# Six PSUM banks as six tiles, and the gate copy ahead of the last exponentials

## The chip, the core and the metric

One core of one Trainium2 chip runs the whole program in one launch. The metric is the device time of one execution in microseconds. PE is TensorE, DVE is VectorE, ACT is ScalarE, POOL is GpSimd, SP is the engine that issues most DMAs.

## What is computed

Block-causal attention over 8 batches of 8 heads (576 positions, head size 64, blocks of 64), then a layer of 8 experts of which each row takes the one with the highest logit:

```
scores = (q @ k.T) / 8                       # per batch and head, 576 x 576
scores = where(i // 64 >= j // 64, scores, -1e9)
attn = exp(scores - max(scores)); attn /= sum(attn) + 1e-9
x = (attn @ v), heads side by side           # 4608 rows of 512
logits = x @ w_gate + modality_bias[modality_id]
e = argmax(logits);  gate = softmax(logits)[e]
out[row] = gate * (relu(x[row] @ w1[e]) @ w2[e])
```

## The kernel before, in words

**Attention.** Two heads of a batch form a pair; there are 32 pairs, and one slot of the program's order handles one. Queries are cut into nine subtiles of 64 rows (subtile s sees 64 (s + 1) keys), and both heads of the pair lie side by side on the 128 partitions. The scores of all nine subtiles fill six PSUM banks, which are one tile, `wide`, of 6 x 512 columns; `COL` (line 48) gives each subtile's first column. Subtile 8 lies across two banks.

The order of the instructions on every engine is written by hand: `ORDER` (line 62) lists the steps of a slot, each with the stage it belongs to (0: this slot's pair, 1: the pair before, -2: a load two pairs ahead). The steps are

- S0 to S3, the scores of a piece (line 188, PE); M0 to M4, the negated maxima of a unit of subtiles (line 193, DVE); E0 to E4, the exponentials (line 199, ACT). E4 handles subtiles 3, 8 and 1.
- G, nine small matmuls of the values with the gate's weights (line 221, PE), and g, the copy of their result out of PSUM next to the values (line 224, ACT). L loads queries and keys two pairs ahead (line 169, SP); values and their transposes come by lines 173 and 174.
- Va and Vb, the attention weights of the pair before times its values (line 233, PE): Va subtiles 0 to 6, Vb 7 and 8. Vb writes the bank that G wrote, and waits for g. Za and Zb normalize their results (lines 245 to 248, DVE).
- T0 to T6, transposes of the exponentials in groups of up to four (line 209, PE), each group into one of the six banks, and C0 to C6, the copies out (line 214; 1, 3 and 5 on DVE, the others on ACT).
- the q steps place the routing of a finished batch between them, a step or two at a time.

The scheduling layer that turns this into a program puts in the waits. It does so by tiles and what is known of each access to them.

**Experts.** `Experts` takes rows in groups of 256: `fetch` gathers them (line 620, POOL), `turn_rows` transposes them (line 633) and splits them in a high and a low part (636 ACT, 637 DVE), `up_products` makes four groups of 24 products (line 651), each evicted by `up_relu` (657 ACT, 658 DVE), `down` makes two groups of 24 (line 697), which line 699 (ACT) scales and line 700 (POOL) scatters. A step is one such group of rows. There are nine steps of the first expert, eight and a short one of the second, one of the third. The products rotate over banks 0 to 2, the turns over banks 3 and 4, and the second `down` group uses bank 5.

Of the kernel before, what the change touches and what calls it, by code (L numbers as in the profile page):

```python
# [11 lines left out]
F32 = mybir.dt.float32  # L12
F32R = mybir.dt.float32r
BF16 = mybir.dt.bfloat16
I32 = mybir.dt.int32
AF = mybir.ActivationFunctionType
ALU = mybir.AluOpType
AX = mybir.AxisListType
# [4 lines left out]
B, H, S, D = 8, 8, 576, 64  # L23
# [3 lines left out]
NSUB = S // D  # L27
# [17 lines left out]
GATE = (NSUB - SEVEN) * VW  # L45
TABLE = GATE + 5 * 2 * NE
UNITS = ((7,), (6, 0), (5,), (4, 2), (3, 8, 1))
COL = {7: 0, 6: 512, 0: 960, 5: 1024, 4: 1536, 2: 1856, 3: 2048, 8: 2304, 1: 2880}
FLIP = (6, 0, 5, 4, 2)
PIECES = (((7, 0, 512),), ((6, 0, 448), (0, 0, 64)), ((5, 0, 384), (3, 0, 256)), ((8, 0, 256), (4, 0, 320), (8, 256, 576), (2, 0, 192), (1, 0, 128)))  # L50
OFF = [32 * s * (s + 1) for s in range(NSUB)]
# [8 lines left out]
PARTS = (("idf", (128,)), ("ii", (128,)), ("iom8", (NE,)), ("iom40", (5, NE)), ("iov40", (5, NE)), ("inv5", (5,)), ("first5", (NE, 5)), ("base8", (NE,)), ("edges", (N // SLOT,)))  # L60

ORDER = (
# [3 lines left out]
)  # L66

# [35 lines left out]
def attention_moe(ctx, tc, qk, vr, vt, gmw, mid, mb, w1, w2, cf, ci, ld, out):  # L103
    nc = tc.nc
    pe, act, dve, pool = nc.tensor, nc.scalar, nc.vector, nc.gpsimd
# [14 lines left out]
    gm = cst.tile([128, PPB, 2 * NE], F32, name="gm")  # L120
    scratch = cst.tile([128, 1024], F32, name="scratch")
    zeros = scratch[:, 0:256].bitcast(BF16)
    lead = cst.tile([128, 128], BF16, name="lead")
    ones = cst.tile([128, 128], BF16, name="ones")
    run = cst.tile([128, NE], F32, name="run")
# [3 lines left out]
    bias = cst.tile([128, B * 5, NE], F32, name="bias")  # L129
# [8 lines left out]
    sml = ctx.enter_context(tc.tile_pool(name="sml", bufs=4, side="right"))  # L138
    att = att_stack.enter_context(tc.tile_pool(name="att", bufs=1, side="right"))
    ps = ctx.enter_context(tc.tile_pool(name="ps", bufs=1, space=PSUM))  # L140

    wide = ps.tile([128, 6 * 512], F32, name="wide")
    banks = [wide[:, 512 * i : 512 * i + 512] for i in range(6)]
    o0, b0 = (ps.tile([128, 512], F32, name=n) for n in ("o0", "b0"))
    raws = [att.tile([128, 2 * S], F32, name=f"raw{i}") for i in range(2)]
    q8s = [att.tile([128, S], F32, name=f"q8{i}") for i in range(2)]
# [29 lines left out]
    def scale(p):  # L176
        d = pairs[p]
        (pool if p else dve).tensor_scalar(d.q, d.raw[:, 0:S], SCALE, None, ALU.mult)  # L178

    def scores(p, u):  # L180
        d = pairs[p]
        if u == 0:
            d.nm = sml.tile([128, NSUB], F32, name="nm")
        for s, a, b in PIECES[u]:
            for h in range(2):
                t = h ^ (s in FLIP)
                hs = slice(64 * h, 64 * h + 64)
                pe.matmul(wide[64 * t : 64 * t + 64, COL[s] + a : COL[s] + b], d.q[hs, D * s : D * s + D], d.k[hs, a:b], start=True, stop=True)  # L188

    def maxima(p, u):  # L190
        d = pairs[p]
        for s in UNITS[u]:
            dve.tensor_reduce(d.nm[:, s : s + 1], wide[:, COL[s] : COL[s] + D * (s + 1)], AX.X, ALU.max, negate=True)  # L193

    def exps(p, u):
        d = pairs[p]
        for s in UNITS[u]:
            n = D * (s + 1)
            act.activation(d.pm[:, OFF[s] : OFF[s] + n], wide[:, COL[s] : COL[s] + n], AF.Exp, bias=d.nm[:, s : s + 1], scale=1.0)  # L199

    def height(g):
        return 64 if g >= HALF else 128
# [199 lines left out]
    def emit(name, p):  # L402
        one = {
            "L": lambda: load(p), "G": lambda: gates(p), "g": lambda: keep_gates(p), "Va": lambda: values(p, 0, SEVEN), "Vb": lambda: values(p, SEVEN, NSUB),
            "Za": lambda: rows(p, o0, 0, SEVEN), "Zb": lambda: rows(p, b0, SEVEN, NSUB),
        }
        if name in one:
            one[name]()
        else:
            dict(S=scores, M=maxima, E=exps, T=transposes, C=copies)[name[0]](p, int(name[1:]))  # L410
# [441 lines left out]
```

## Time and profile before

| what | value |
|---|---|
| median of 3 runs (lowest, highest) | 1529.61 us (1524.93, 1530.62) |
| the profiled run's own time | 1524.37 us |
| its span | 1522.6 us |
| PE busy with matmuls | 1033.8 us, 68% of the span |
| DVE, ACT, POOL busy | 380.8, 315.8, 216.5 us |
| mean granted TensorE clock | 0.784 |

Times inside the profile are microseconds from the start of the span. The granted clock is a share of 2.4 GHz: 1.00 is 2.4 GHz, 0.50 is 1.2 GHz. "Idle before" a group is the time in which its engine did nothing just before its instructions, and behind the arrow stands what ended that time.

### The profile page before, as it was taken

How to read it: one execution, taken by the hardware profiler on the slowest of the kernel's cores; microseconds unless marked ns; L12 is line 12 of the kernel's file. 1: busy time of each engine (PE TensorE's matmuls, PEld its weight loads, DVE VectorE, ACT ScalarE, POOL GpSimd, SP SyncE). 2: the span in 40 equal slices, each digit the busy share in tenths (PEclk: the TensorE clock that was granted, in tenths of full speed). 3: DMA queues.
4: the chain of work that ended last, by engine and by line, in shares of the span. 5: the costliest groups of instructions: out<-in, count | busy, mean ns of one | idle time of the engine just before them, and what ended most of it. 6: DMA issues, size and time to landing. Idle time of an engine off the chain costs nothing. (4 is left out here: it accounts for less than half of the span.)

```text
span 1522.6 us, 20688 instructions
## 1 busy us (share of the span) xinstructions
PE 1033.8 (68%) x8696; PEld 775.3 (51%) x8696; DVE 380.8 (25%) x995; ACT 315.8 (21%) x622; POOL 216.5 (14%) x177
## 2 busy tenths in 40 slices
PE   5656666556666665666656677777777777777776
PEld 2434434334344343343433466666666666666665
DVE  2322322323323233243322322111111111111110
ACT  2222222222222222222222211111111111111111
POOL 1000000101001010012242004111211111110100
PEclk6765666766657676666766779999999999999989
DMA  3123213113113113124333012111121011111000
GB/s 105 56 66 105 63 37 81 51 33 88 44 35 94 35 49 80 36 60 110 99 94 96 4 46 53 42 49 42 44 68 42 29 56 49 49 56 35 23 14 17
DMA packets 82623, 85.11 MB, mean 56 GB/s; under 512 B 53002, under 2 KB 64970, under 8 KB 82528
## 3 DMA queue, kind: packets, MB, share of 16 engines
q1 hardware_dynamic: 75040, 64.24, 15.5%
q0 software_dynamic: 7488, 19.52, 4.0%
q8 instruction: 69, 1.13, 0.3%
q14 instruction: 26, 0.21, 0.0%
HBM read 62.09 MB, written 22.25 MB: 55 GB/s over the span
## 5 line engine op out<-in xcount | busy, mean ns | idle before, releaser
L209 PE MATMUL wide<-cf,pm 128*128 128x128 f32 (+1 forms) x800 | 176.9, 353 | 152.7 <-DVE pt L214 81.6
L188 PE MATMUL wide<-raw,q 64*64 64x256 f32 (+7 forms) x1280 | 193.7, 689 | 122.4 <-ACT pm L199 113.2
L209 PEld LDWEIGHTS wide<-cf,pm 128*128 128x128 f32 (+1 forms) x800 | 103.7, 163 | 219.4 <-DVE pt L214 114.9
L193 DVE TENSOR_REDUCE nm<-wide 128x1 f32<-128x512 f32 (+8 forms) x288 | 129.6, 487 | 338.6 <-PE wide L188 286.8
L199 ACT ACTIVATE pm<-wide,nm 128x512 f32<-128x512 f32 (+8 forms) x288 | 138.0, 525 | 360.9 <-DVE nm L193 352.4
L188 PEld LDWEIGHTS wide<-raw,q 64*64 64x64 f32 x1280 | 84.9, 208 | 226.1 <-ACT pm L199 158.2
L651 PE MATMUL wide<-extra 128*128 128x256 f32 x960 | 127.4, 290 | 47.6 <-DVE extra L658 40.0
L658 DVE SCALAR_TENSOR_TENSOR extra<-wide,extra 128x512 fp32r<-128x512 f32 x72 | 49.8, 692 | 437.6 <-ACT extra L657 437.6
L178 POOL TENSOR_SCALAR q<-raw 128x576 f32<-128x576 f32 x31 | 51.2, 1650 | 689.3 <-DMA raw<-qk 666.1
L651 PEld LDWEIGHTS wide<-extra 128*128 128x128 f32 x960 | 119.5, 194 | 56.9 <-DVE extra L658 45.7
L214 ACT COPY pt<-wide 128x512 f32<-128x512 f32 (+1 forms) x128 | 64.5, 504 | 312.0 <-PE wide L209 312.0
L651 PE MATMUL wide<-extra,w0hb 128*128 128x256 f32 x512 | 95.7, 287 | 40.6 <-DVE extra L658 34.4
L214 DVE COPY pt<-wide 128x512 f32<-128x512 f32 (+1 forms) x96 | 66.1, 689 | 209.3 <-PE wide L209 209.3
L651 PEld LDWEIGHTS wide<-extra,w0hb 128*128 128x128 f32 x512 | 78.2, 188 | 48.9 <-DVE extra L658 39.2
L233 PE MATMUL o<-v,pt 128*64 128x73 f32 x2048 | 99.7, 267 | 0.0
L657 ACT ACTIVATE extra<-wide 128x512 fp32r<-128x512 f32 x72 | 43.0, 597 | 267.4 <-PE wide L651 266.6
L233 PEld LDWEIGHTS o<-v,pt 128*64 128x64 f32 x2048 | 94.9, 168 | 0.1
L233 PE MATMUL b<-v,pt 128*64 128x73 f32 x1152 | 44.8, 232 | 62.7 <-ACT v L224 62.7
L233 PEld LDWEIGHTS b<-v,pt 128*64 128x64 f32 x1152 | 40.0, 139 | 67.3 <-ACT v L224 67.3
L651 PE MATMUL wide<-extra,w0lb 128*128 128x256 f32 x256 | 71.7, 280 | 0.0
L697 PE MATMUL o<-extra 128*128 128x512 f32 x240 | 66.2, 436 | 0.0
L633 PE MATMUL wide<-cf,xr 128*128 128x128 f32 x148 | 33.0, 362 | 48.2 <-DVE extra L637 23.8
(142 smaller groups left out, 923.2 us busy)
## 6 DMA issues: line engine op xcount, KB each, us to landing
raw<-qk SPq DMA_DIRECT2D x31, 576.0 KB, 3.8
v<-vr SPq DMA_DIRECT2D x32, 320.0 KB, 3.8
vt<-vt SPq DMA_DIRECT2D x32, 288.0 KB, 4.0
xrows<-xr SPq DMA_DIRECT2D x16, 576.0 KB, 5.6
staging<-w SPq DMA_DIRECT2D x24, 256.0 KB, 4.5
staging<-w SPq DMA_DIRECT2D x12, 512.0 KB, 3.7
idlist<-btmp SPq DMA_DIRECT2D x8, 304.0 KB, 5.3
idlist<-idt,pi POOLq DMA_INDIRECT x40, 2.2
```

The costliest lines, as they stand in the source:

```text
L178: (pool if p else dve).tensor_scalar(d.q, d.raw[:, 0:S], SCALE, None, ALU.mult)
L188: pe.matmul(wide[64 * t : 64 * t + 64, COL[s] + a : COL[s] + b], d.q[hs, D * s : D * s + D], d.k[hs, a:b], start=True, stop=True)
L193: dve.tensor_reduce(d.nm[:, s : s + 1], wide[:, COL[s] : COL[s] + D * (s + 1)], AX.X, ALU.max, negate=True)
L199: act.activation(d.pm[:, OFF[s] : OFF[s] + n], wide[:, COL[s] : COL[s] + n], AF.Exp, bias=d.nm[:, s : s + 1], scale=1.0)
L209: pe.transpose(banks[GBANK[g]][0:m, 128 * i : 128 * i + 128], d.pm[:, o : o + m], idf)
L214: dve.tensor_copy(dst, src) if g in ON_DVE else act.copy(dst, src)
L233: pe.matmul(o[64 * h : 64 * h + 64], d.pt[:, a : a + 64], d.v[:, 5 * h + j, :], start=j == 0, stop=j == s // 2)
L633: nc.tensor.transpose(x[:, n * a + 128 * i : n * a + 128 * i + 128], s.xg[:, i, 128 * kc : 128 * kc + 128], self.idf)
L651: nc.tensor.matmul(hp[:, a, :], w[:, kc, ms], x[:, kc, :], start=i == 0, stop=i == len(mm) - 1)
L657: self.nc.scalar.activation(hh, hp, AF.Relu)
L658: self.nc.vector.scalar_tensor_tensor(hl, hp, 0.0, hh, ALU.max, ALU.subtract)
L697: nc.tensor.matmul(y, s.hs[m][x][:, ts], self.part(w, 1, m // 2)[:, m % 2, :], start=n == 0, stop=n == len(mm) - 1)
```

## The change

The six banks become six tiles, `bank0` to `bank5`, in the same places; `COL` names a bank and an offset in it. An instruction can then no longer reach over two banks, so subtile 8 is cut at key 256: its maximum is a reduction over the first 256 columns into a spare column of `nm`, and then one `tensor_scalar` over the other 320 that takes the smaller of the two negated maxima; its exponential is two instructions. The matmuls stay what they were: subtile 8 was already written in two pieces. In `ORDER`, E4 moves from ahead of G to behind g, so that ACT copies the gate's terms before the last exponentials.

```diff
-COL = {7: 0, 6: 512, 0: 960, 5: 1024, 4: 1536, 2: 1856, 3: 2048, 8: 2304, 1: 2880}
+COL = {7: (0, 0), 6: (1, 0), 0: (1, 448), 5: (2, 0), 4: (3, 0), 2: (3, 320), 3: (4, 0), 8: (4, 256), 1: (5, 320)}
+CUT = 256
 ...
-    ("S0", 0), ("S1", 0), ("M0", 0), ("qv", 1), ("E0", 0), ("S2", 0), ("M1", 0), ("E1", 0), ("S3", 0), ("M2", 0), ("E2", 0), ("M3", 0), ("E3", 0), ("M4", 0), ("E4", 0),
-    ("G", 0), ("L", -2), ("q1", 1), ("Va", 1), ("g", 0), ("q2", 1), ("q3", 1), ("Vb", 1), ("Za", 1), ("q4", 1), ("Zb", 1),
+    ("S0", 0), ("S1", 0), ("M0", 0), ("qv", 1), ("E0", 0), ("S2", 0), ("M1", 0), ("E1", 0), ("S3", 0), ("M2", 0), ("E2", 0), ("M3", 0), ("E3", 0), ("M4", 0),
+    ("G", 0), ("L", -2), ("q1", 1), ("Va", 1), ("g", 0), ("E4", 0), ("q2", 1), ("q3", 1), ("Vb", 1), ("Za", 1), ("q4", 1), ("Zb", 1),
 ...
+    dump = scratch[:, 256:512].bitcast(BF16)
 ...
-    wide = ps.tile([128, 6 * 512], F32, name="wide")
-    banks = [wide[:, 512 * i : 512 * i + 512] for i in range(6)]
+    banks = [ps.tile([128, 512], F32, name=f"bank{i}") for i in range(6)]
 ...
+    def place(s, a, b):
+        i, o = COL[s] if a == 0 else (COL[s][0] + 1, -CUT)
+        return banks[i][:, o + a : o + b]
+
+    def spans(s):
+        n = D * (s + 1)
+        return [(0, n)] if n <= 512 else [(0, CUT), (CUT, n)]
 ...
-                pe.matmul(wide[64 * t : 64 * t + 64, COL[s] + a : COL[s] + b], d.q[hs, D * s : D * s + D], d.k[hs, a:b], start=True, stop=True)
+                pe.matmul(place(s, a, b)[64 * t : 64 * t + 64], d.q[hs, D * s : D * s + D], d.k[hs, a:b], start=True, stop=True)
 ...
-            dve.tensor_reduce(d.nm[:, s : s + 1], wide[:, COL[s] : COL[s] + D * (s + 1)], AX.X, ALU.max, negate=True)
+            for a, b in spans(s):
+                low = d.nm[:, s : s + 1] if b == D * (s + 1) else d.nm[:, NSUB : NSUB + 1]
+                if a == 0:
+                    dve.tensor_reduce(low, place(s, a, b), AX.X, ALU.max, negate=True)
+                else:
+                    dve.tensor_scalar(dump[:, 0 : b - a], place(s, a, b), -1.0, d.nm[:, NSUB : NSUB + 1], ALU.mult, ALU.min, accum_out=low)
 ...
-            n = D * (s + 1)
-            act.activation(d.pm[:, OFF[s] : OFF[s] + n], wide[:, COL[s] : COL[s] + n], AF.Exp, bias=d.nm[:, s : s + 1], scale=1.0)
+            for a, b in spans(s):
+                act.activation(d.pm[:, OFF[s] + a : OFF[s] + b], place(s, a, b), AF.Exp, bias=d.nm[:, s : s + 1], scale=1.0)
```

What the built programs say of it is shown at three places on PE, with the waits that each instruction carries (the name in brackets is the engine or queue whose earlier work it waits for; line numbers of the changed kernel are 9 to 14 higher). The first is T0 to T6 of one slot, before:

```order
L209 MATMUL wide<-cf,pm_102 128x128 x4
L209 MATMUL wide<-cf,pm_102 128x128 [waits Activation_49]
L209 MATMUL wide<-cf,pm_102 128x128 x3
L209 MATMUL wide<-cf,pm_102 128x128 [waits DVE_49]
L209 MATMUL wide<-cf,pm_102 128x128 x3
L209 MATMUL wide<-cf,pm_102 128x128 [waits Activation_49]
L209 MATMUL wide<-cf,pm_102 128x128 x3
L209 MATMUL wide<-cf,pm_102 128x128 [waits DVE_49]
L209 MATMUL wide<-cf,pm_102 128x128 x3
L209 MATMUL wide<-cf,pm_102 64x128 [waits Activation_49]
L209 MATMUL wide<-cf,pm_102 64x128 x3
L209 MATMUL wide<-cf,pm_102 64x128 [waits DVE_49]
```

and of the changed kernel:

```order
L223 MATMUL bank_90<-cf,pm_108 128x128 x4
L223 MATMUL bank_91<-cf,pm_108 128x128 x4
L223 MATMUL bank_92<-cf,pm_108 128x128 x4
L223 MATMUL bank_93<-cf,pm_108 128x128 [waits Activation_49]
L223 MATMUL bank_93<-cf,pm_108 128x128
L223 MATMUL bank_93<-cf,pm_108 128x128 [waits Activation_49]
L223 MATMUL bank_93<-cf,pm_108 128x128
L223 MATMUL bank_94<-cf,pm_108 128x128 x3
L223 MATMUL bank_94<-cf,pm_108 128x128 [waits Activation_49]
L223 MATMUL bank_95<-cf,pm_108 64x128 x4
L223 MATMUL bank_90<-cf,pm_108 64x128 [waits Activation_49]
```

Before, each group carried a wait for the copy of the group ahead of it (ACT and DVE in turn). Now T0 to T2 carry none; the three waits in T3 and T4 are for exponentials of E4, and T6 waits for C0, which empties the bank it writes. The second place is S0 to S3, before:

```order
L188 MATMUL wide<-raw_93,q_95 64x512 [waits DMAHW1_49,Activation_49,Pool_49]
L188 MATMUL wide<-raw_93,q_95 64x512
L188 MATMUL wide<-raw_93,q_95 64x448 x2
L188 MATMUL wide<-raw_93,q_95 64x64 x2
L188 MATMUL wide<-raw_93,q_95 64x384 [waits Activation_49]
L188 MATMUL wide<-raw_93,q_95 64x384
L188 MATMUL wide<-raw_93,q_95 64x256 x2
L188 MATMUL wide<-raw_93,q_95 64x256 [waits Activation_49]
L188 MATMUL wide<-raw_93,q_95 64x256
L188 MATMUL wide<-raw_93,q_95 64x320 x4
L188 MATMUL wide<-raw_93,q_95 64x192 x2
L188 MATMUL wide<-raw_93,q_95 64x128 x2
```

and of the changed kernel:

```order
L197 MATMUL bank_90<-raw_98,q_100 64x512 [waits DMAHW1_49,Activation_49,Pool_49]
L197 MATMUL bank_90<-raw_98,q_100 64x512
L197 MATMUL bank_91<-raw_98,q_100 64x448 [waits DVE_49]
L197 MATMUL bank_91<-raw_98,q_100 64x448
L197 MATMUL bank_91<-raw_98,q_100 64x64 x2
L197 MATMUL bank_92<-raw_98,q_100 64x384 x2
L197 MATMUL bank_94<-raw_98,q_100 64x256 x4
L197 MATMUL bank_93<-raw_98,q_100 64x320 [waits DVE_49]
L197 MATMUL bank_93<-raw_98,q_100 64x320
L197 MATMUL bank_95<-raw_98,q_100 64x320 [waits DVE_49]
L197 MATMUL bank_95<-raw_98,q_100 64x320
L197 MATMUL bank_93<-raw_98,q_100 64x192 x2
```

Before, S2 waited for E0 and S3 for E1, both of the same slot. Now the waits are for the slot before: C6 (bank 0), C1, C3 and C5 (banks 1, 3 and 5). The third place is an expert step: four groups of products and a turn, before:

```order
L651 MATMUL wide<-extra 128x256 [waits Activation_49]
L651 MATMUL wide<-extra 128x256 x23
L651 MATMUL wide<-extra 128x256 [waits DVE_49]
L651 MATMUL wide<-extra 128x256 x23
L651 MATMUL wide<-extra 128x256 [waits DVE_49]
L651 MATMUL wide<-extra 128x256 x23
L651 MATMUL wide<-extra 128x256 [waits DVE_49]
L651 MATMUL wide<-extra 128x256 x23
L633 MATMUL wide<-cf,xr_79 128x128 [waits DMASW0_49,DVE_49]
L633 MATMUL wide<-cf,xr_79 128x128 [waits DMASW1_49]
L633 MATMUL wide<-cf,xr_79 128x128 x2
L633 MATMUL wide<-cf,xr_79 128x128 [waits DVE_49]
```

and of the changed kernel:

```order
L665 MATMUL bank_92<-extra 128x256 x17
L665 MATMUL bank_90<-extra 128x256 x24
L665 MATMUL bank_91<-extra 128x256 x24
L665 MATMUL bank_92<-extra 128x256 [waits DVE_49]
L665 MATMUL bank_92<-extra 128x256 x23
L647 MATMUL bank_93<-cf,xr_79 128x128 [waits DMASW5_49]
L647 MATMUL bank_93<-cf,xr_79 128x128 [waits DMASW6_49]
L647 MATMUL bank_93<-cf,xr_79 128x128 x2
L647 MATMUL bank_94<-cf,xr_79 128x128 x4
```

Before, every group waited for the eviction of the group ahead of it, and the second turn for that of the first. Now a group waits only for the eviction of the bank it writes, three groups back, and the turns for their rows alone.

## Rows read from the trace of the kernel before

**Rows 1.** The page, part 2: the granted TensorE clock in 40 slices of the span, in tenths.

```profile
PEclk6765666766657676666766779999999999999989
```

**Rows 2.** The page, part 5: groups by line. Line, engine, operation, tiles, form, count | busy us, mean ns of one | idle time of the engine just before, and what ended most of it.

```profile
L209 PE MATMUL wide<-cf,pm 128*128 128x128 f32 (+1 forms) x800 | 176.9, 353 | 152.7 <-DVE pt L214 81.6
L188 PE MATMUL wide<-raw,q 64*64 64x256 f32 (+7 forms) x1280 | 193.7, 689 | 122.4 <-ACT pm L199 113.2
...
L193 DVE TENSOR_REDUCE nm<-wide 128x1 f32<-128x512 f32 (+8 forms) x288 | 129.6, 487 | 338.6 <-PE wide L188 286.8
L199 ACT ACTIVATE pm<-wide,nm 128x512 f32<-128x512 f32 (+8 forms) x288 | 138.0, 525 | 360.9 <-DVE nm L193 352.4
...
L651 PE MATMUL wide<-extra 128*128 128x256 f32 x960 | 127.4, 290 | 47.6 <-DVE extra L658 40.0
...
L233 PE MATMUL b<-v,pt 128*64 128x73 f32 x1152 | 44.8, 232 | 62.7 <-ACT v L224 62.7
```

**Rows 3.** The timeline of PE over one slot, from the end of the slot before. Start, length, instructions [idle before <- what ended it].

```profile
416.95 0.42 PE L209 MATMUL wide<-cf,pm 128*64 128x128 f32 x1 [0.84 <-DVE pt L214]
...
417.76 1.98 PE L188 MATMUL wide<-raw,q 64*64 64x512 f32 x12 [0.29 <-issue]
421.37 1.55 PE L188 MATMUL wide<-raw,q 64*64 64x384 f32 x8 [1.63 <-ACT pm L199]
424.83 2.61 PE L188 MATMUL wide<-raw,q 64*64 64x256 f32 x20 [1.91 <-ACT pm L199]
427.37 1.14 PE L221 MATMUL b<-gm,vt 128*64 128x16 f32 x17
...
428.43 3.62 PE L233 MATMUL o<-v,pt 128*64 128x73 f32 x63
433.41 1.37 PE L233 MATMUL b<-v,pt 128*64 128x73 f32 x36 [1.36 <-ACT v L224]
...
436.10 0.66 PE L209 MATMUL wide<-cf,pm 128*128 128x128 f32 x4 [0.73 <-ACT pt L214]
```

**Rows 4.** The timeline of PE: the first score matmuls of the first two slots, and the first work after the last transposes of the last of the 32 slots.

```profile
5.69 1.10 PE L188 MATMUL wide<-raw,q 64*64 64x512 f32 x12
...
31.18 1.98 PE L188 MATMUL wide<-raw,q 64*64 64x512 f32 x12 [0.40 <-issue]
...
882.40 1.11 PE L633 MATMUL wide<-cf,xr 128*128 128x128 f32 x4 [0.35 <-ACT pt L214]
```

**Rows 5.** Windows: stretch, its length, then busy time of PE, PE's weight loads, DVE, ACT and POOL with counts, the granted clock, the mean busy share of the 16 DMA engines, GB/s. The first score pieces of the program, two parts of the slot of rows 3, and a stretch of the last slot.

```profile
5.69:9.21 3.52, 1.96 (x21) 0.69 (x20) 0.69 (x1) 0.69 (x1) 1.11 (x1) 1.00 1.07 332
417.60:424.60 7.00, 3.53 (x20) 1.10 (x20) 1.68 (x5) 1.41 (x4) 0.00 (x0) 0.50 0.00 0
431.60:437.60 6.00, 3.06 (x57) 2.35 (x53) 3.48 (x15) 2.08 (x5) 3.49 (x3) 1.00 0.25 56
897.09:906.52 9.43, 9.43 (x152) 9.35 (x151) 3.41 (x13) 0.60 (x1) 0.00 (x0) 1.00 0.40 96
```

**Rows 6.** The timeline of PE over one expert step, from its third group of products to the next step's third.

```profile
1099.71 3.13 PE L651 MATMUL wide<-extra 128*128 128x256 f32 x24 [1.41 <-DVE extra L658]
...
1108.81 0.66 PE L633 MATMUL wide<-cf,xr 128*128 128x128 f32 x4 [1.41 <-DVE extra L658]
1110.87 1.11 PE L633 MATMUL wide<-cf,xr 128*128 128x128 f32 x4 [1.40 <-DVE extra L637]
1111.64 6.83 PE L697 MATMUL o<-extra 128*128 128x512 f32 x24
1118.31 5.60 PE L697 MATMUL wide<-extra 128*128 128x512 f32 x24
1124.68 3.14 PE L651 MATMUL wide<-extra 128*128 128x256 f32 x24 [0.78 <-ACT scratch L699]
...
1133.84 3.13 PE L651 MATMUL wide<-extra 128*128 128x256 f32 x24 [1.41 <-DVE extra L658]
```

**Rows 7.** The timeline of PE in the last slot, where attention's last values stand between the first expert's products.

```profile
897.09 2.27 PE L233 MATMUL o<-v,pt 128*64 128x73 f32 x64
...
900.44 3.14 PE L651 MATMUL wide<-extra 128*128 128x256 f32 x24
...
903.56 3.12 PE L651 MATMUL wide<-extra 128*128 128x256 f32 x24
906.52 3.14 PE L697 MATMUL o<-extra 128*128 128x512 f32 x13
909.49 0.62 PE L633 MATMUL wide<-cf,xr 128*128 128x128 f32 x4
909.87 1.84 PE L697 MATMUL o<-extra 128*128 128x512 f32 x7
```

**Rows 8.** Windows over four slots each (columns as in rows 5), the second with the staging of weights, and the DMA issues of the queries and keys (count, KB each, median us from issue to landing).

```profile
245.00:352.00 107.00, 64.30 (x714) 41.57 (x716) 34.31 (x96) 25.35 (x56) 10.35 (x8) 0.68 0.22 57
672.00:780.00 108.00, 66.80 (x740) 44.14 (x736) 38.51 (x120) 25.94 (x57) 31.80 (x21) 0.69 0.35 92
...
raw<-qk SPq DMA_DIRECT2D x31, 576.0 KB, 3.8
```

**Rows 9.** Groups by line and form: the smallest exponential and the smallest maximum.

```profile
L199 ACT ACTIVATE pm<-wide,nm 128x64 f32<-128x64 f32 x32 | 9.8, 307 | 0.0
...
L193 DVE TENSOR_REDUCE nm<-wide 128x1 f32<-128x64 f32 x32 | 6.9, 215 | 0.0
```

More of the change, by code (lines that the diff above doesn't have):

```diff
@@ L182, in scores @@
         if u == 0:
-            d.nm = sml.tile([128, NSUB], F32, name="nm")
+            d.nm = sml.tile([128, NSUB + 1], F32, name="nm")
         for s, a, b in PIECES[u]:
```

## Prediction

> **What bounds the kernel now.** I read the page first, then the groups by line, then the timeline of one slot, then the timeline of one expert step. The span is 1522.6 us; the profiled run took 1524.37, so 1.8 lies outside the span, and the median of the three runs, 1529.61, is 5.2 above the profiled one. The sum below is made against 1524.4. The page's slices [rows 1] show two halves: up to slice 23 TensorE's clock is granted at about 0.65 on average, later at 0.9 or more. No engine is full in the first half. The groups by line say who keeps PE idle there [rows 2]: PE stands idle for 152.7 us before transposes, 81.6 of it until a VectorE copy out of PSUM is done, and for 122.4 us before scores, 113.2 of it until an exponential is done. Neither is a need of the data. A transpose writes one PSUM bank while a copy reads another.
>
> The timeline shows the same in one slot [rows 3]. The second group of transposes, at 436.10, finds PE idle for 0.73 us until the copy of the first is done. The scores stop likewise after 1.98 us until the first exponentials are done (1.63 idle), and again before the third piece (1.91). So PE, VectorE and ScalarE take turns. A slot goes from one first score to the next; from 31.18 to 882.40 there are 31 of them [rows 4], 27.46 us each. The windows [rows 5] add the second loss: after such turns the granted clock is 0.50, which is 1.2 GHz, and after the long unbroken run of matmuls from 424.83 on it is 1.00, 2.4 GHz. In the expert steps a group of 24 products is 3.1 us long, with 1.41 us of idle time before it [rows 6], again until an eviction from another bank is done.
>
> **What the change does to this, part by part.** The built program (the sections on the change above) shows the waits gone: in a slot the groups of transposes follow one another with waits only for exponentials, and the last for its own bank; the scores wait only for their own bank's last copy, and the expert's four products run on. So from here I price an unbroken PE.
>
> *An attention slot.* S: the first slot ran its first 1024 of 2880 score columns in 1.10 us at 2.4 GHz [rows 4, 5], so all of them take 3.1. G takes 1.06 (from 427.37 to 428.43, [rows 3]). Va and Vb run unbroken in the last slot, from 897.09 to 900.44: 3.35 [rows 7]; the window over that stretch was granted 1.00 [rows 5]. Transposes: there four start 0.38 before what follows them (909.49 to 909.87, [rows 7]), so six groups are 2.3. The last one needs the bank of the next score, so its copy C6 stays in the path: from its start, 416.95, to the next first score, 417.76, it is 0.81 [rows 3]. Sum 10.6 us, against 27.46.
>
> Does anything else end later? DVE: maxima 129.6 / 32 = 4.05 us a slot; ScalarE: exponentials 138.0 / 32 = 4.31 [rows 2]. If M0 starts 0.7 after the slot's first score and the others follow without a gap, the maxima end near 5.2, and the last exponentials some 1.6 later, near 6.8. The first transpose that needs them (the fourth group) is due near 3.1 + 1.06 + 3.35 + 3 x 0.38 = 8.7. So this chain has 2 us to spare. DVE is busy for 34.31 us in 107 [rows 8], 8.8 a slot, of 10.6: nearly full, but inside. POOL and the loads: the raw load lands 3.8 us after its issue [rows 8] and is issued more than a slot ahead. The DMA engines' mean share of 0.22 is 6.0 us a slot, and 0.35, or 9.6, where weights are staged too [rows 8]; both fit in 10.6, the second barely.
>
> *The split of subtile 8.* One maximum and one exponential more a slot. Its ends: nothing, since PE covers them (2 us to spare), and one whole small instruction each, 0.215 and 0.307 by the 64-column forms [rows 9], 32 x 0.52 = 17 us. I take nothing.
>
> *The gate copy ahead of E4.* PE waited 62.7 us before Vb for it [rows 2]. In the new slot E3 ends near 4.5, G at 4.2, so the copy is done at about 4.9 and Vb is due at 6.4: this wait goes. It is within the 27.46, so it is not counted again. Behind the copy on ScalarE now stand E4 and C0, and the copy waits for G, whose vt load is issued over a slot ahead: no cost while that holds.
>
> I take 11.0 a slot rather than 10.6, since the routing's few matmuls and extra DVE work come in every fourth slot, and 2 us more for each of the four staging slots: 31 x 11.0 + 8 = 349. The stretch took 851.2: **502 saved**. The bounds are 10.4 (no leftover waits, less tail in S) and 13 a slot, 322 to 403.
>
> *Slot 0* took 25.5 us [rows 4] and cannot go below a later slot, so 0 to 15 can be saved; its loads hold it, I take **10**.
>
> *An expert step* takes 34.13 us (from the third group of products at 1099.71 to the next step's at 1133.84): four groups of products, two turns, two down groups. Unbroken, a product group follows another after 2.96 (903.56 to 906.52), four transposes take 0.38, a down group 5.6 when the clock is full (1118.31, [rows 6, 7]). 4 x 2.96 + 2 x 0.38 + 2 x 5.6 = 23.8; I take 24.0. Of the 10.1 saved 7.8 are idle time (0.78 + 3 x 1.41 + 1.41 + 1.40), the rest is pipeline fill and the clock, which falls when the turns come (the first down group takes 6.67 against 5.6). Sixteen such steps give **162**. The last slot, the short step and the step of the third expert hold the same waits; I count them as 1.7 steps: **17**. What is late next in a step? The last hidden pieces are ready 1.4 after the fourth product, and the down group needs them only for its last quarter, 4 us in. The gathers and weight loads have 24 us where they need 4.
>
> Sum: 502 + 10 + 162 + 17 = 691; 1524.4 - 691 = 833. I forecast **835 us**, with 805 to 880 if its mechanism holds (slots of 10.4 to 12.5).
>
> **Rivals.**
>
> *The clock stays low in attention.* PE then needs twice what it needs at 2.4 GHz for S, V and the transposes, 6.2, 6.7 and 4.6, and the same 1.06 and 0.81: 19.4 a slot. 31 x 8.1 less 8, or 243, is saved there, and with 5 + 179 the time is 1097. For it: the present slots. Against it: the idle left is one gap of about 0.6 in 11 us, while the expert steps keep 0.9 of the clock or more in most slices [rows 1] with 1.41 idle in 4.55. The Trainium skill, "TensorE: Matmul & The Clock Gate", section "A second HAM failure mode: psum-queue depth-cycling", speaks for it: a kernel that cycles through PSUM banks pauses briefly between groups, and its clock swings between the two levels. By that rule the time would be this rival's. The unbroken stretch from 897.09, which passes through several banks, was granted 1.00, which speaks against the rule here [rows 5, 7]. 5 in 100.
>
> *Another engine becomes the bound.* DVE has 8.8 of 10.6 us and the same order; if its evictions wait behind Za and Zb, or staging DMA and POOL slow it, a slot is 14, not 11: 31 x 3 = 93 more, 926. For it: the small margin and one DVE instruction more. Against it: the 2 us to spare at the fourth transposes, and of DVE's three copies none stands between the last transposes and the next first score. 14 in 100.
>
> *The waits are not where the time goes, and only the gate copy works.* If PE were held by something that the wait names merely accompany, the gain is at most the 62.7 before Vb: 1462. Against it: the trace names the copy as what ends PE's idle time before each group, and the matmuls' own time fills only 10.6 of 27.46. 2 in 100.
>
> *Slower.* The gate copy now stands ahead of E4 and waits for G, and G for the vt load. If vt lands late, PE, E4 and C0 all stop, where E4 ran on before. To lose more than the 691 won, each slot must wait 22.6 us more for a load that lands some 4 us after its issue. At 23 us a slot it is 34 long, and the time 1524.4 - 189 + 31 x 6.54 = 1538. 1 in 100.
>
> **How the numbers follow.** Forecast 78 in 100, the rivals 5, 14, 2 and 1. The range of 8 in 10 reaches from 805 to 935, which takes in the bounds of the forecast and most of the rival with another bound. A measurement can tell about 0.5%, 8 us, from no change. Everything but the last rival lies far below, so faster 0.97, the same 0.01, slower 0.02, the last two a little above their cases for what I have not thought of.
>
> **What would show it.** Right: first scores 11 us apart; no idle time of PE before transposes but the last; PE's clock 9 in all slices after the first; the expert's products 2.96 apart and steps of 24; Vb without a wait. Wrong: a clock row of 5 or 6 in the attention slices (first rival); PE waiting for DVE copies or exponentials in the fourth transposes group (second); the old 1.4 between groups (third); G waiting for a DMA (fourth).

## The result, and the profile after

The changed kernel takes 789.97 us (788.80 to 790.35), the kernel before 1528.27 us (1524.93 to 1530.62) on the same chip. The ratio is 0.517, with an interval of 0.5157 to 0.5181: much faster, and below the range given, whose low end was 805. The profiled execution took 790.35 us with a span of 788.7.

The page, part 2: busy tenths of PE and DVE and the granted clock in 40 slices of the span, which answers to [rows 1].

```profile
PE   8999999999989888799999999999999999999995
...
DVE  6888888888879867654122111122212222212120
...
PEclk9999999999999999899999999999999999999998
```

The granted clock is 0.9 or more in all slices but two, and PE is busy nearly throughout. DVE is at eight tenths in the attention half. The groups by line (line, form, count | busy us, mean ns | idle before, and what ended it) show the waits of [rows 2] gone:

```profile
L665 PE MATMUL bank<-extra 128*128 128x256 f32 x960 | 117.7, 283 | 0.6 <-DVE extra L651 0.3 <-ACT extra L650 0.2
L223 PE MATMUL bank<-cf,pm 128*128 128x128 f32 (+1 forms) x800 | 94.8, 275 | 0.4 <-ACT pm L213 0.4
L197 PE MATMUL bank<-raw,q 64*64 64x256 f32 (+7 forms) x1280 | 91.5, 426 | 19.9 <-POOL q L179 10.9 <-issue 8.9
...
L247 PE MATMUL b<-v,pt 128*64 128x73 f32 x1152 | 44.5, 227 | 1.3 <-issue 1.3
```

The idle time before transposes (L223) fell from 152.7 us to 0.4, before scores (L197) from 122.4 to 19.9, before the products shown (L665) from 47.6 to 0.6, and before the Vb matmuls from 62.7 to 1.3. What is left before the scores is new: 10.9 us wait for POOL, which scales the queries. Before scores, transposes and Vb together 337.8 us of idle time became 21.6, which is 9.9 of the 17.6 us by which a slot became shorter. The rest is time of the matmuls themselves: the same 800 transposes had 353 ns each and have 275. A regular slot in the timeline of PE (start, length, instructions, idle before), which answers to [rows 3]:

```profile
162.76 2.70 PE L197 MATMUL bank<-raw,q 64*64 64x512 f32 x40 [0.40 <-issue]
165.39 0.70 PE L235 MATMUL b<-gm,vt 128*64 128x16 f32 x17
165.88 0.28 PE L247 MATMUL o<-v,pt 128*64 128x73 f32 x1
165.94 0.21 PE L235 MATMUL b<-gm,vt 128*64 128x16 f32 x1
166.00 2.17 PE L247 MATMUL o<-v,pt 128*64 128x73 f32 x62
168.00 0.23 PE L247 MATMUL b<-v,pt 128*64 128x73 f32 x1
168.01 0.22 PE L247 MATMUL o<-v,pt 128*64 128x73 f32 x1
168.06 1.32 PE L247 MATMUL b<-v,pt 128*64 128x73 f32 x35
169.32 2.95 PE L223 MATMUL bank<-cf,pm 128*128 128x128 f32 x25
172.10 0.34 PE L288 MATMUL b<-l,cf 128*128 128x72 f32 x2
172.66 2.70 PE L197 MATMUL bank<-raw,q 64*64 64x512 f32 x40 [0.22 <-issue]
```

The 40 score matmuls and the 25 transposes each stand as one unbroken run, and the slot takes 9.90 us where it took 27.46. On the other engines the order of the change is seen in the same slot: DVE does the two parts of subtile 8's maximum, and ACT the gate copy (L238) between the exponentials.

```profile
163.95 3.14 DVE L205 TENSOR_REDUCE nm<-bank 128x1 f32<-128x512 f32 x8 [0.90 <-PE bank L197]
167.21 0.55 DVE L207 TENSOR_SCALAR_CACHE_REDUCE scratch<-bank,nm 128x320 bf16<-128x320 f32 x1
```

```profile
164.67 2.78 ACT L213 ACTIVATE pm<-bank,nm 128x512 f32<-128x512 f32 x6 [2.01 <-DVE nm L205]
167.32 0.26 ACT L238 COPY v<-b 128x80 f32<-128x80 f32 x1
167.43 1.59 ACT L213 ACTIVATE pm<-bank,nm 128x256 f32<-128x256 f32 x4
```

The last exponential ends at 169.02, 6.26 after the slot's first score, before the first transpose at 169.32. The windows (columns as in [rows 5]) over ten slots and over the last staging slots:

```profile
13.82:113.00 99.18, 95.85 (x1838) 85.07 (x1838) 83.34 (x261) 63.02 (x152) 23.23 (x16) 1.00 0.63 173
...
290.00:330.00 40.00, 31.04 (x543) 26.44 (x541) 29.02 (x79) 19.12 (x46) 27.76 (x19) 0.88 0.72 203
```

In the first PE is busy for 97% of the time at full clock; in the second for 78%, with POOL at 69% and the DMA engines at 0.72. Not all slots are regular. The timeline of PE at the first two scores, the last two, and the work after them, which answers to [rows 4]:

```profile
5.99 2.70 PE L197 MATMUL bank<-raw,q 64*64 64x512 f32 x40
...
13.82 2.69 PE L197 MATMUL bank<-raw,q 64*64 64x512 f32 x40 [0.46 <-issue]
...
329.43 4.41 PE L197 MATMUL bank<-raw,q 64*64 64x512 f32 x40 [5.24 <-POOL q L179]
...
340.99 1.09 PE L647 MATMUL bank<-cf,xr 128*128 128x128 f32 x8 [0.35 <-ACT pt L228]
```

Slot 0 takes 7.83 us; the slot before 329.43 takes 17.2, with 5.24 of idle time until POOL has scaled the queries. Who made POOL late stands in the DMA issues of SP and the work of POOL just ahead of it:

```profile
318.22 1.28 SPq L605 DMA_DIRECT2D staging<-w  x2
319.60 0.52 SPq L170 DMA_DIRECT2D raw<-qk  x1
```

```profile
319.25 2.36 POOL L614 TENSOR_TENSOR extra<-staging,extra 128x1024 fp32r<-128x1024 f32 x1
327.72 1.65 POOL L179 TENSOR_SCALAR q<-raw 128x576 f32<-128x576 f32 x1 [6.11 <-DMA raw<-qk]
```

The load of queries is issued behind two staging loads and lands some 8 us later, and POOL stands idle for 6.11 us for it. The wait costs more than itself, as the window over the scores behind it shows:

```profile
329.43:333.77 4.34, 4.34 (x41) 2.44 (x41) 2.05 (x6) 1.24 (x3) 3.30 (x4) 0.60 0.31 75
```

After the idle time the granted clock is 0.60, and the scores take 4.34 us in place of 2.63. An expert step, which answers to [rows 6]:

```profile
370.19 11.76 PE L665 MATMUL bank<-extra 128*128 128x256 f32 x96
381.78 1.04 PE L647 MATMUL bank<-cf,xr 128*128 128x128 f32 x8
382.57 5.72 PE L711 MATMUL o<-extra 128*128 128x512 f32 x24
388.13 5.60 PE L711 MATMUL bank<-extra 128*128 128x512 f32 x24
393.57 11.08 PE L665 MATMUL bank<-extra 128*128 128x256 f32 x91
```

All 96 products are one run of 11.76 us, and a step takes 23.38 us where it took 34.13.

### The profile page after: what moved, and what is told of

It is laid out like the page before. It is cut to its first block, busy times and chain, and to the rows that moved or that the text cites. A ratio compares the mean times of both kernels' runs of the same rounds, so it can differ in the third digit from the quotient of the medians.

```text
span 788.7 us, 20741 instructions
## 1 busy us (share of the span) xinstructions
PE 752.3 (95%) x8696; PEld 670.4 (85%) x8696; DVE 369.3 (47%) x1059; ACT 306.5 (39%) x654; POOL 216.5 (27%) x177
## 5 line engine op out<-in xcount | busy, mean ns | idle before, releaser
L213 ACT ACTIVATE pm<-bank,nm 128x320 f32<-128x320 f32 (+3 forms) x320 | 138.1, 507 | 89.7 <-DVE nm L205 88.2
L205 DVE TENSOR_REDUCE nm<-bank 128x1 f32<-128x256 f32 (+7 forms) x288 | 111.2, 446 | 39.4 <-PE bank L197 39.2
L665 PE MATMUL bank<-extra 128*128 128x256 f32 x960 | 117.7, 283 | 0.6 <-DVE extra L651 0.3
L665 PEld LDWEIGHTS bank<-extra 128*128 128x128 f32 x960 | 116.6, 192 | 1.7 <-DVE extra L651 0.5
L197 PE MATMUL bank<-raw,q 64*64 64x256 f32 (+7 forms) x1280 | 91.5, 426 | 19.9 <-POOL q L179 10.9
L197 PEld LDWEIGHTS bank<-raw,q 64*64 64x64 f32 x1280 | 61.3, 138 | 49.0 <-issue 31.5
L223 PE MATMUL bank<-cf,pm 128*128 128x128 f32 (+1 forms) x800 | 94.8, 275 | 0.4 <-ACT pm L213 0.4
L665 PE MATMUL bank<-extra,w0hb 128*128 128x256 f32 x512 | 91.2, 281 | 0.0
L223 PEld LDWEIGHTS bank<-cf,pm 128*128 128x128 f32 (+1 forms) x800 | 85.8, 135 | 3.3 <-ACT pm L213 0.8
L228 ACT COPY pt<-bank 128x512 f32<-128x512 f32 (+1 forms) x128 | 62.7, 505 | 46.1 <-PE bank L223 46.1
L665 PEld LDWEIGHTS bank<-extra,w0hb 128*128 128x128 f32 x512 | 79.1, 188 | 0.7
L665 PE MATMUL bank<-extra,w0lb 128*128 128x256 f32 x256 | 71.9, 281 | 0.0
L711 PEld LDWEIGHTS bank<-extra 128*128 128x128 f32 x240 | 45.1, 188 | 9.3
```

Of the source, the lines that this page charges most:

```text
L197: pe.matmul(place(s, a, b)[64 * t : 64 * t + 64], d.q[hs, D * s : D * s + D], d.k[hs, a:b], start=True, stop=True)
L205: dve.tensor_reduce(low, place(s, a, b), AX.X, ALU.max, negate=True)
L213: act.activation(d.pm[:, OFF[s] + a : OFF[s] + b], place(s, a, b), AF.Exp, bias=d.nm[:, s : s + 1], scale=1.0)
L223: pe.transpose(banks[GBANK[g]][0:m, 128 * i : 128 * i + 128], d.pm[:, o : o + m], idf)
L228: dve.tensor_copy(dst, src) if g in ON_DVE else act.copy(dst, src)
L665: nc.tensor.matmul(hp[:, a, :], w[:, kc, ms], x[:, kc, :], start=i == 0, stop=i == len(mm) - 1)
```

## The experiments

**Theory:** waits went by tile; the six banks were one tile, so PE, DVE and ACT took turns; with six tiles PE runs unbroken at full clock and is itself the bound. **Rivals:** the gate copy's place makes the gain; another engine is just behind PE; the banks themselves collide.

The first four kernels below ran beside a kernel before of 1526.6 us, about what it took beside the changed kernel (1528.27), so they are compared with the 790 above. The others ran on two other chips: the next four on one on which the kernel before took 1549.04 and the changed kernel was not run, the last four, the changed kernel among them, on one on which the kernel before took 1552.22.

**Split only.** The changed kernel with the old `ORDER`:

```diff
-("M4", 0), ("G", 0), ("L", -2), ("q1", 1), ("Va", 1), ("g", 0), ("E4", 0),
+("M4", 0), ("E4", 0), ("G", 0), ("L", -2), ("q1", 1), ("Va", 1), ("g", 0),
```

> The six tiles and the cut of subtile 8 stay, the order of the steps goes back: E4 stands ahead of G and g again. My theory: then Vb waits for g, and g stands behind E4 on ScalarE. In the slot of the changed kernel E4 would end near 6.8 us after the slot's first score, g near 7.1, and Vb is due at about 5.3, so PE loses some 1.6 us a slot, 31 x 1.6 = 50: about 840 us, and the idle time before the Vb matmuls is some 50 us. Rival: with the banks apart ScalarE is far enough ahead, and the order of E4 and g costs nothing: 790 us.

Measured: 819.27 us (817.33 to 822.08), 29 more than with both parts. The groups by line name the wait that was expected:

```profile
L247 PE MATMUL b<-v,pt 128*64 128x73 f32 x1152 | 43.9, 229 | 32.9 <-ACT v L238 32.9
```

It is 0.96 us in a regular slot, and the slot 11.07 us in place of 9.90; I had estimated 1.6, which only some slots with routing reach. So the tiles alone bring 707 of the 737 us, and the order matters once the tiles are apart: the gate copy is due when the exponentials are not done.

**Move only.** The kernel before with the new `ORDER`, which is the same edit the other way round.

> The kernel before (one tile of six banks, subtile 8 uncut) with the new order alone: g ahead of E4. My theory: the 62.7 us that PE waited for g go, but the first group of transposes then waits for E4, which is later by the same step, so part comes back: about 1485 us, with new idle time before the first transposes. Rivals: the whole wait goes, 1465 us; or it only changes its name, 1528 us. The clock stays near 0.65 in the attention slices in all three.

Measured: 1489.45 us (1485.38 to 1492.24), 37 less than the kernel before. The groups of transposes show the part that comes back:

```profile
L209 PE MATMUL wide<-cf,pm 128*128 128x128 f32 (+1 forms) x800 | 188.4, 371 | 181.1 <-DVE pt L214 81.2 <-ACT pt L214 66.5 <-ACT pm L199 32.5
...
L233 PE MATMUL b<-v,pt 128*64 128x73 f32 x1152 | 44.3, 227 | 0.0
```

The 62.7 us before Vb are gone; the transposes' idle time grew from 152.7 to 181.1, with 32.5 of it now ended by exponentials. 62.7 - 28.4 = 34 us, near the 37. The third rival of the prediction (only the gate copy works) is out.

**Two tiles of three banks**, subtile 8 uncut, the new order:

```diff
-    banks = [ps.tile([128, 512], F32, name=f"bank{i}") for i in range(6)]
+    whole = [ps.tile([128, 512 * n], F32, name=f"whole{i}") for i, n in enumerate((3, 3))]
+    banks = [w[:, o : o + 512] for w, n in zip(whole, (3, 3)) for o in range(0, 512 * n, 512)]
```

> The changed order, but two tiles of three banks each in place of six tiles; subtile 8 uncut, no instruction reaches over the two tiles. The program then waits between two banks of one tile: the second, third, fifth and sixth group of transposes each wait for the copy of the group ahead, the third score piece for the first exponentials, and all product groups of the experts for the eviction ahead. My theory (waits go by tile, and the waits are the cost): the 179 us of the expert steps stay lost, and of the attention slots 4 waits of 1.3 and one of 1.6, 31 x 6.8 = 211: about 1180 us, 1100 to 1300 with what the clock does. Rival (any split breaks the chain of turns): near 800 us. Rival (the banks themselves collide, the tiles only name it): as the changed kernel or as the one before, with the same gaps wherever two engines touch two banks.

Measured: 1169.54 and 1184.32 us at a granted clock of 0.920 and 0.895, and 1197.56 and 1198.97 at 0.872 and 0.875. The first two are 0.782 (0.7767 to 0.7872) of the kernel before. The timeline of PE in the execution of 1169.54 us shows waits where two banks share a tile:

```profile
299.85 0.66 PE L215 MATMUL whole<-cf,pm 128*128 128x128 f32 x4 [0.73 <-ACT pt L220]
301.36 1.68 PE L215 MATMUL whole<-cf,pm 128*128 128x128 f32 x8 [0.85 <-DVE pt L220]
303.82 1.12 PE L215 MATMUL whole<-cf,pm 128*128 128x128 f32 x4 [0.79 <-DVE pt L220]
305.65 1.28 PE L215 MATMUL whole<-cf,pm 128*64 128x128 f32 x5 [0.72 <-ACT pt L220]
307.38 1.98 PE L194 MATMUL whole<-raw,q 64*64 64x512 f32 x12 [0.45 <-issue]
310.99 3.48 PE L194 MATMUL whole<-raw,q 64*64 64x384 f32 x28 [1.62 <-ACT pm L205]
```

The rows are the second group of transposes, the third with the fourth, the fifth, and the sixth with the last, then the scores in two parts. The fourth, the first in the second tile, runs on behind the third as one row of eight; the second, third, fifth and sixth each wait for the copy of the group ahead in their own tile. That the banks collide is out too: in the changed kernel copies read some banks while PE writes others, and nothing waits. The windows of two slots of this one kernel separate the waits from the clock:

```profile
307.38:327.49 20.11, 15.29 (x185) 11.09 (x186) 8.07 (x22) 6.46 (x14) 3.65 (x3) 0.67 0.40 102
345.22:362.10 16.88, 10.87 (x186) 8.42 (x186) 8.65 (x26) 6.34 (x14) 1.65 (x1) 1.00 0.31 77
```

With the same work the slot takes 16.88 us at a granted 1.00 and 20.11 at 0.67. So the waits, with the fill behind each, cost 16.88 - 9.90 = 7.0 us a slot (I had 6.8), and the lower clock 3.2 more where it is 0.67. The expert steps, which I had left at their old length, take 30.2 us and not 34.13, since the first turn and the first product group of a step find their own tile free there. That the total came near the 1180 expected is thus part luck: attention lost 249 us against the changed kernel (584.1 from the first score to the experts, where that has 335.0) and not 211, and the experts less than 179.

**Experts on one bank.** All product groups use bank 0; attention is untouched.

```diff
     def s_bank(self):
         self.sbank += 1
-        return self.banks[(self.sbank - 1) % 3]
+        return self.banks[0]
```

In the first 256 rows the third product group's sums are overwritten by the fourth's before they are evicted; no other rows change.

> The changed kernel, but all product groups of the experts use bank 0, so each group waits for the eviction of the one ahead again; the attention slots stay as they are. My theory (a wait of 1.4 us each before the groups, the term of the expert steps): 3 to 4 waits x 1.4 in some 18 steps, 75 to 100, about 870 us, attention unchanged at 9.9 us a slot; steps of 28 to 29 us in place of 23.4, and the granted clock still 0.95 or more there. Rival (the down groups or the gathers set the step): about 800 us. Rival (the clock falls after the gaps as in the kernel before, and turns the loss into that of the kernel before): 10 us a step, 950 us.

Measured: 884.38 us (883.44 to 886.48), 94 more. The timeline of PE:

```profile
406.32 3.03 PE L665 MATMUL bank<-extra 128*128 128x256 f32 x24
410.77 3.14 PE L665 MATMUL bank<-extra 128*128 128x256 f32 x24 [1.41 <-DVE extra L672]
415.32 3.13 PE L665 MATMUL bank<-extra 128*128 128x256 f32 x24 [1.41 <-DVE extra L672]
419.87 3.14 PE L665 MATMUL bank<-extra 128*128 128x256 f32 x24 [1.41 <-DVE extra L672]
```

A step takes 28.3 us, 4.95 more: three waits of 1.41 and 0.24 of fill behind each. The granted clock of the whole run is 0.986, so these gaps alone do not lower it. The regular attention slots stay at 9.90.

**Banks 4 and 5 as one tile**, subtile 8 uncut; the edit is that of the two tiles, with other sizes:

```diff
-    whole = [ps.tile([128, 512 * n], F32, name=f"whole{i}") for i, n in enumerate((3, 3))]
+    whole = [ps.tile([128, 512 * n], F32, name=f"whole{i}") for i, n in enumerate((1, 1, 1, 1, 2))]
```

> The changed kernel with banks 4 and 5 as one tile, so that subtile 8 needs no cut: one maximum and one exponential fewer a slot, and the sixth group of transposes waits for the copy of the fifth. My theory: the cut costs nothing, PE covers it, and the new wait costs about 0.6 to 1.2 us a slot less what the last group waits anyway: 790 to 815 us. Rival (VectorE, 83% busy, or ScalarE sets the slot): without the cut each saves 0.2 to 0.3 us a slot, 780 to 785 us.

Measured: 821.44 us (819.40 to 823.61), above the 790 to 815 expected. The changed kernel did not run on that chip; by the ratios to the kernel before, 0.5303 here and 0.5169 and 0.5133 for the changed kernel on two other chips, the shared tile costs 21 to 26 us. The timeline of PE (the slot is 10.87 us):

```profile
163.21 2.40 PE L215 MATMUL whole<-cf,pm 128*128 128x128 f32 x20
166.34 0.73 PE L215 MATMUL whole<-cf,pm 128*64 128x128 f32 x5 [0.73 <-ACT pt L220]
```

One fewer maximum and exponential gain nothing that shows; one shared tile costs 0.97 us a slot, 0.73 as a wait. I had thought that the last group's own wait would swallow a part of it. The cut of subtile 8 thus pays: its two extra instructions cost nothing that shows, and it makes the sixth tile possible.

**What bounds the changed kernel.** Two kernels each take away one loss that its profile shows, a third both. The last transpose goes to bank 2, so that the next slot's first score need not wait for its copy; and the staging steps of slots 26 to 29 both stand at T0, behind the slot's load of queries and keys:

```diff
-GBANK = (0, 1, 2, 3, 4, 5, 0)
+GBANK = (0, 1, 2, 3, 4, 5, 2)
```

```diff
-    (26, "S0"): ("prep",), (26, "T0"): ("prep",),
+    (26, "T0"): ("prep", "prep"),
...
-    (29, "S0"): ("prep",), (29, "T0"): ("prep",),
+    (29, "T0"): ("prep", "prep"),
```

> The changed kernel, with the last transpose (T6) written to bank 2 in place of bank 0, so that the next slot's first score no longer waits for its copy C6. My theory (PE alone sets the slot, and the 0.40 us before each first score are this wait): 31 x 0.4 = 12 less, about 777 us, first scores 9.5 us apart. Rival (VectorE, POOL or a load sets the slot just behind PE): the idle time moves to another wait and the time stays at 790 us. Rival: T6 now waits longer for C2, which empties bank 2, and loses up to 0.4 a slot: 800 us.

> The changed kernel, but in slots 26 to 29 both weight staging steps are issued at T0, behind the load of queries and keys, where one of them stood at S0, ahead of it. My theory (the last slots are long because that load is issued late, behind staging transfers that wait on SP for POOL, and the scaled queries come late): the longest slots, 17.2 and 12.6 us, go to 11 to 12, 10 to 17 us less: 773 to 780 us. Rival (the DMA engines, 0.87 busy there, or POOL set those slots): the load only moves, 787 to 792 us. Rival (staging now collides with the transposed-value loads): 795 us or more.

> Both edits of the two kernels beside it: the last transpose in bank 2, and both staging steps behind the load of queries and keys. My theory (two separate losses on PE's path): their gains add, 760 to 768 us. Rival (they share a bound): no better than the better of the two.

Measured: 786.91 (784.87 to 789.36), 787.08 (786.25 to 791.75) and 774.20 us (773.12 to 774.97). Beside 790 the first two looked like almost nothing, though their slots were shorter as expected; but they ran on the chip of 1549.04, without the changed kernel. So the three ran again on the chip of 1552.22, beside it:

> The changed kernel once more, beside the three kernels that follow, on one chip with them, since they first ran on another chip than it, where the kernel before was 1.5% slower and PE lost some 5 us in the first full expert step with its instructions coming in fours. If that loss belongs to the chip: about 795 us wherever the gaps show, 790 us where they don't. If it belongs to the three kernels: 790 us and no gaps here, and the gaps in the others.

> The last transpose in bank 2, once more, on one chip with the changed kernel. By its slots (9.43 us against 9.90) it should gain 31 x 0.45 = 14 us. My theory from the first run: the gain up to slot 24 is kept (about 11 us), but the slots with staging grow (POOL's scaled queries come late by a load that stands behind staging), so 5 to 11 us less than the changed kernel: 779 to 785 beside 790. Rival: no gain at all beside it.

> Both staging steps behind the load, once more, on one chip with the changed kernel. By the slots of its first run it should gain 11.8 us; if the gaps in the first expert step are the chip's, the whole of that shows: 778 beside 790. If they are its own: 4 to 7 us, 784 beside 790.

> Both edits, once more, on one chip with the changed kernel: 24.5 us less by the slots of its first run, so 766 beside 790; if the gaps in the first expert step are its own, 770.

Measured:

| kernel | us (lowest, highest) | ratio to before, interval | first to last first-score |
|---|---|---|---|
| changed kernel | 797.36 (795.26, 798.54) | 0.5133 (0.5114 to 0.5152) | 322.13 |
| last transpose in bank 2 | 785.85 (784.35, 786.76) | 0.5060 (0.5042 to 0.5079) | 311.40 |
| loads ahead of staging | 785.73 (783.60, 795.12) | 0.5070 (0.5044 to 0.5095) | 310.54 |
| both | 775.03 (774.12, 777.57) | 0.4992 (0.4974 to 0.5010) | 298.35 |

The first two gain 11.5 and 11.6 us, both together 22.3: the losses are separate, and the gains add. I had expected 5 to 11, 11.8 and 24.5. Regular slots with bank 2 are 9.43 us. So PE was the bound there. 31 x 0.45 = 14 would have been the gain; the trace of that kernel loses a part again in slots with staging (13.08 us where the changed kernel has 11.91). Both edits together give a version 2.8% faster than the changed kernel on the same chip (775.03 / 797.36 = 0.972).

## Why the prediction was wrong

The mechanism and the forecast's case were right, and so was the sign. What failed is the size of terms of the sum: S and G in the regular slot (3.1 and 1.06 us, measured 2.63 and 0.61), slot 0 (10 saved, measured 17.7) and the expert step (24.0, measured 23.35). They erred to the same side, and most had no range of their own. Of the profiled runs' own times, 1524.4 and 790.4, 734 us were saved, where the sum had 691.

| term | forecast saved | measured | how measured |
|---|---|---|---|
| 31 slots | 502 | 524 | 851.2 - 327.2 (13.82 to 340.99) |
| slot 0 | 10 | 17.7 | 25.5 - 7.83 |
| 16 expert steps | 162 | 172 | 16 x (34.13 - 23.35) |
| last slot, short step, third expert | 17 | 20 | the rest |

**The regular slot** was put at 11.0 us and is 9.90. Three parts of it failed. S was 3.1 and is 2.63 (162.76 to 165.39): the step that scaled 1.10 us for 1024 columns took a group's displayed length for its share of PE, but what follows begins before that length is over. In the changed kernel's slot the timeline up to 163.65 already counts 13 score matmuls, and the same 1024 columns are 12 of them [rows 4], so what follows them begins at most 0.89 us after the first; and the 2.70 us row at 162.76 and the row at 165.39 overlap. G was 1.06 and is 0.61 (165.39 to 166.00): I took it from a stretch of [rows 3] in which the clock was still low, though the sum assumed 1.00. I had put the clock at 1.00 from 424.83 on; the windows over the last scores (424.83 to 427.37) and over G show 0.50:

```profile
427.37:428.43 1.06, 1.06 (x22) 1.06 (x21) 0.56 (x1) 0.28 (x1) 0.00 (x0) 0.50 0.00 0
```

The allowance of 0.4 for routing is 0.13 in the slots that have it (10.03). V was right (3.35 forecast, 3.32 measured, from 166.00 to 169.32). The tail from the first transpose to the next score was 3.1 and is 3.34.

**The staging slots** failed in the other direction: 8 us were added for four of them, and all irregular slots together cost 327.2 - 31 x 9.90 = 20. The rival of another bound was right in this one place, by a way that it did not name: the load of queries, in SP's queue behind staging loads that themselves wait for POOL. I had found the loads more than a slot ahead in a slot of 27 us, and did not go through SP's queue again for slots of 10. The loads-first kernel shows the cause: with the load ahead, the 16.92 us slot becomes 11.33. A part of the 20 is the clock: the scores behind POOL's wait ran at 0.60.

**Slot 0** "cannot go below a later slot" was false by the code: its pair has no V before it. It is 7.83 us, about a later slot less the 3.4 of V and plus its own waits.

**An expert step** is 23.3 to 23.4 us and not 24.0. The terms gave 23.8, and I rounded up. Four groups were priced at 11.84, from a single group that other work follows, and all 96 products issue in 11.59 (370.19 to 381.78). Two down groups were priced at their displayed length, 11.2, and take 11.0 (382.57 to 393.57). The one-bank kernel shows the price of the wait right: 1.41 and 0.24 of fill.

**The range** was built by moving the slot alone. With 31 slots at the lowest slot that I allowed, 10.4, and the rest as forecast, the time is about 807; the mean slot, with the irregular ones, was 327.2 / 31 = 10.55, inside. What carried the result below 805 was the error of all the terms that had no range of their own.

**The rivals.** The clock did not stay low: 1.00 over ten slots. The Trainium skill, "TensorE: Matmul & The Clock Gate", section "A second HAM failure mode: psum-queue depth-cycling", tells of a bf16 kernel that cycles through PSUM banks, pauses briefly and often between its groups, and swings between the two levels. The changed kernel cycles through six banks without the pauses, and its trace shows no such swing (0.988 granted over the run), so the cycling alone does not bring it here. The kernel of two tiles does swing, with slots at 0.67 and slots at 1.00, and it has a wait before nearly every group. Which idle time lets the clock fall, the runs don't settle: the one-bank kernel was granted 1.00 over its first expert steps (406 to 460) with 1.41 idle before each of three groups in four.

**DVE** had room: 8.3 us a slot of 9.92 in the ten-slot window, close to the 8.8 of the forecast, and its last maximum ends 5.2 us after the first score, as forecast, though it starts them at 1.2 and not at 0.7, so that this agreement is part luck. But little is left: with slots of 9.43 it is the next candidate, and the runs did not test it. **The slower case** did not come: G waits for a load only in slot 0. (Its 22.6 us a slot should have been 691 / 31 = 22.3.)

## What to carry to other kernels

A tile is the unit of waiting. Where independent buffers are slices of one tile, look in the trace for one engine's matmuls waiting for another's copy out of a different slice, and split the tile at that boundary, also where an instruction has to be cut for it. To price a stage that will run unbroken, measure from start to start at the clock that you forecast, never from the length of a group; and give every term of a large sum its own range, since errors from one habit point one way. When a stage shrinks to a third, go through the queues of its loads again: what was a slot ahead is now late.

## What the runs showed of the hardware that was not expected

On the chip on which the kernel before took 1552.22 us, the same changed kernel took 797.36 in place of 789.97. The timeline of PE in its first full expert step there shows most of the difference:

```profile
380.74 0.62 PE L665 MATMUL bank<-extra 128*128 128x256 f32 x3 [0.22 <-issue]
382.17 0.99 PE L665 MATMUL bank<-extra 128*128 128x256 f32 x5 [0.82 <-issue]
383.61 0.99 PE L665 MATMUL bank<-extra 128*128 128x256 f32 x4 [0.44 <-issue]
```

Matmuls come in threes to fives, here 1.43 us apart, with nothing that the profile shows to wait for, and the step takes 29.26 us where it took 23.48 beside the kernel before of 1528.27. Later steps are equal in both profiles, at 23.3 to 23.4. The same pattern stands in this step of every kernel that was profiled on that chip and on the one of 1549.04, five kernels in eight profiles. It is absent from the changed kernel and the split-only kernel in the profiles taken beside a kernel before of 1527 to 1528 us. What PE's sequencer waited for there is open. For the comparison of kernels it means that a difference of 1% wants the kernel it is compared with on the same chip.
